# Key differences of the row maximum taken from stacked halves of k and from q over minus q, and q's row pairs added by a reduction

## The chip, the cores and the metric

The kernel runs on one core of a Trainium2 chip. The core has TensorE (PE; its weight loads are listed as PEld), VectorE (DVE), ScalarE (ACT), GpSimd (POOL), and SyncE (SP), whose queue starts nearly all DMAs here. The metric is the device time of one execution in microseconds, the median of several runs.

## The reference

```python
def _attn_ref(q, k, v):                       # (4, 8, 1152, 64) each
    q_pool = q.reshape(B, H, S // 2, 2, D).mean(axis=3)
    scores = scale * np.matmul(q_pool, k.transpose(0, 1, 3, 2))
    scores = scores - np.max(scores, axis=-1, keepdims=True)
    attn = np.exp(scores)
    attn = attn / (np.sum(attn, axis=-1, keepdims=True) + 1e-09)
    return np.matmul(attn, v)
def _moe_ref(x, w_gate, w_noise, noise, w1, w2):   # x (2304, 512), 8 experts, F = 1024
    noisy_logits = x @ w_gate + np.log1p(np.exp(x @ w_noise)) * noise
    top2 = ...                                # two experts per row, weights by softmax
    out[mask] += top2_w * (np.maximum(x[mask] @ w1[e], 0.0) @ w2[e])
```

q's rows are averaged in pairs, so 576 query rows of each of the 32 heads meet 1152 keys. The output of attention feeds a mixture of experts.

## The kernel before, in words

Two batch items of one head form a *pair*; there are 16, each with 1152 query rows (9 chunks of 128; the middle one, c = 4, holds the end of the first item and the start of the second) and 18 key chunks. A pair's rows are worked on in three *segments* of three chunks, 48 segments in all.

Values that need more than fp16 are split into a high half (`hi`, ScalarE, L293) and a low one (`lo`, VectorE, L290: scaled source minus high half). For a pair: SP loads the keys into `kr` (L267) and q into `qr` (L279 to L282). ScalarE and VectorE write high and low half of the keys side by side into `kn`, and a DMA transposes `kn` into `kt` (L296), so that partitions 0 to 63 of `kt` hold the high half and 64 to 127 the low one. `kt`'s upper rows are copied within SBUF into `kt2` (L454). For q, an add of the two rows of each pair gives `qs` (L462, on GpSimd or VectorE), ScalarE writes its high half twice side by side into `qn`, in one instruction, and this is transposed into `qt` (L296). The low half goes to `qn2`.

The row maximum, needed before exp, doesn't look at each score of its own. Each item's key chunks are taken as two blocks of ND = 4 chunks and one chunk of rest. `kd` is the difference of the two blocks in `kt` (`k_df`, L300, VectorE, two per pair). TensorE forms D = q.kd and S = q.(second block) (`max_mm`, L306); ScalarE writes relu(D) to `rd` (L314), and VectorE adds S and takes the maximum (L318), as max(a, b) = b + relu(a - b). A reduction (L336) adds the rest, and `max_fin` (L343 to L345) writes the negative maximum into two columns of `qn2`, which is transposed into `qt2`. In the order of instructions both this and the first transposition stand as `qt..<-qn..`: `qt_0` and `qt_1` are the buffers of `qt2`, `qn_0` and `qn_1` those of `qn2`.

Then come the scores (L358 with `qt` and `kt`, L359 with `qt2` and `kt2`, which subtracts the maximum too), exp on ScalarE into `pf` (L366), the low half `pl` of the probabilities (L371 on VectorE, one instruction of 128x768, or L374 on GpSimd, two of 128x384), the product with the values (`pv`, L394) and the division (L405 to L416). Routing scatters the rows to buffers of the experts (`xg`), which were filled with zeros from `zt` before (L683).

No instruction's place is written by hand. Class `Plan` (L114) is a list scheduler: each operation has an engine with a cost, a key (when it is wanted), a latency, buffers that it takes and gives back, and a flag `port`; operations with this flag on VectorE and on GpSimd are planned not to overlap. Where two engines are given (the sum of q, `pl`), the planner takes the one that ends first. A pair's operations are due some units before its first segment, a unit being a key chunk of a segment; that lead is 0, -6, -2, 4, 10 and 16 for the first six pairs and 20 from then on. For the first four pairs `qt2` is transposed by segments, later in one piece.

Of the kernel before, what the change touches and what calls it, by code (L numbers as in the profile page):

```python
# [14 lines left out]
ALU = mybir.AluOpType  # L15
AX = mybir.AxisListType
# [3 lines left out]
P = 128  # L20
# [4 lines left out]
NK = 9  # L25
D = 64
# [27 lines left out]
ND = 4  # L54
# [59 lines left out]
class Plan:  # L114
# [17 lines left out]
    def op(s, eng, cost, key, fn, deps=(), lat=None, port=False, take=(), give=(), ready=0.0, gen=None, after=None):  # L132
        o = Op(eng, cost, key, fn, lat, port, take, give)
        o.ready, o.gen = ready, gen
        s.hard += gen is None
        for tag in give:
            s.refs[tag] = s.refs.get(tag, 0) + 1
        for d in deps:
            if d.done is None:
                d.succ.append(o)  # L140
                o.wait += 1
            else:
                o.ready = max(o.ready, d.done)
        if after and after.done is None:
            after.then.append(o)
            o.wait += 1
        if not o.wait:
            s.can.append(o)
        return o
# [70 lines left out]
class Attn:  # L220
# [68 lines left out]
    def lo(s, out, src, scale, hi):  # L289
        s.nc.vector.scalar_tensor_tensor(out, src, scale, hi, op0=ALU.mult, op1=ALU.subtract)  # L290

    def hi(s, out, src, scale):
        s.nc.scalar.activation(out, src, AF.Copy, scale=scale)  # L293

# [1 line left out]
        s.nc.sync.dma_start_transpose(out=out, in_=src.rearrange("p c d -> p (c d)"))  # L296

    def k_df(s, i, h):
        kt = s.G.buf["kt", i].rearrange("p (b c) t -> p b c t", b=2)
        s.nc.vector.tensor_sub(s.G.buf["kd", i][:, h], kt[:, h, 0:ND], kt[:, h, ND:2 * ND])  # L300

# [116 lines left out]
    def pairs(s):  # L418

        G = s.G  # L420
        op = G.op
        B = s.G.buf
        scale = IN_SCALE
# [3 lines left out]
        for i in range(NPAIR):  # L427
            b = 27 * i
            x = i == 0
            ahead = (0, -6, -2, 4, 10, 16)[i] if i < 6 else 20  # L430
            hs = [slice(0, NK), slice(NK, 2 * NK)]
            k = lambda late, first: b - first if x else b - late - ahead * (late > 16)
            lq = []
# [3 lines left out]
            for h in range(2):  # L437
                lk.append(op("SP", 0.6, k(62, 99) + 2 * h, lambda i=i, h=h: s.load_k(i, h), lat=3.0,
                             take=[("kr", ("kr", i))] if h == 0 else (), after=lk[0] if h else None))
            lq.append(op("SP", 2.6, k(60, 95), lambda i=i: s.load_q(i, 1 if i == 0 else 2), lat=3.0,  # L440
                         take=() if x else [("qr", ("qr", i))], after=lq[0] if x else None))
            tr, df, kc = [], [], []
            hi = None
            for h, c in enumerate(hs):
                hi = op("ACT", 0.58, k(50, 90) + 4 * h, lambda i=i, c=c: s.hi(B["kn", i][:, c, 0:D], B["kr", i][:, c], scale),
                        deps=[lk[h]], take=[("kn", ("kn", i)), ("kt", ("kt", i))] if h == 0 else (), after=hi)
                lo = op("DVE", 0.67, k(48, 90) + 4 * h,
                        lambda i=i, c=c: s.lo(B["kn", i][:, c, D:], B["kr", i][:, c], scale, B["kn", i][:, c, 0:D]),
                        deps=[hi], port=True, give=[("kr", i)])
                tr.append(op("SP", 1.3 if x else 1.7, k(47, 90) + 4 * h, lambda i=i, c=c: s.transpose(B["kt", i][:, c], B["kn", i][:, c]),  # L450
                             deps=[lo], lat=2.1 if x else 3.2, give=[("kn", i)]))
                df.append(op("DVE", 0.33, k(38, 80) + 4 * h + 34 * h * x, lambda i=i, h=h: s.k_df(i, h),
                             deps=[tr[h]], port=True, take=[("kd", ("kd", i))] if h == 0 else (), after=df[0] if h else None))
                kc.append(op("SP", 0.6, k(20, 82) + 9 * h, lambda i=i, c=c: s.nc.sync.dma_start(B["kt2", i][0:D, c], B["kt", i][0:D, c]),  # L454
                             deps=[tr[h]], take=[("kt2", ("kt2", i))] if h == 0 else (), after=kc[0] if h else None))
            s.last = lq + tr
            qt, ql, a = [], [], None
            for p in ((0, 1) if x else (2,)):
                c = (slice(0, 3), slice(3, NCQ), slice(0, NCQ))[p]
                f = (c.stop - c.start) / NCQ  # L460
                a = op((("POOL", 0.1 + 1.45 * f), ("DVE", 0.07 + 0.74 * f)), 0, k(50, 92) + 8 * p * x,
                       lambda eng, i=i, c=c: (s.nc.vector if eng == "DVE" else s.nc.gpsimd).tensor_add(  # L462
                           B["qs", i][:, c], B["qr", i][:, c, 0], B["qr", i][:, c, 1]),
                       deps=[lq[p % 2]], port=True, take=[("qs", ("qs", i)), ("qn", ("qn", i)), ("qt", ("qt", i))] if p != 1 else (), after=a,
                       give=[("qr", i)])

                def q_hi(i=i, c=c):
                    m = c.stop - c.start
                    s.hi(B["qn", i][:, c].rearrange("p c (y d) -> p c y d", y=2),
                         B["qs", i][:, c, None, :].to_broadcast([P, m, 2, D]), 0.5 * scale)  # L470
                hi = op("ACT", 0.1 + 0.96 * f, k(44, 91) + 8 * p * x, q_hi, deps=[a])
                t = op("SP", 1.35, k(43, 91) + 8 * p * x, lambda i=i, c=c: s.transpose(B["qt", i][:, c], B["qn", i][:, c]), deps=[hi], lat=2.0 if x else 2.7,
                       give=[("qn", i)])
                qt.append(t)
                ql.append(op("DVE", 0.07 + 0.6 * f, k(40, 45) + 20 * p * x,
                             lambda i=i, c=c: s.lo(B["qn2", i][:, c, 0:D], B["qs", i][:, c], 0.5 * scale, B["qn", i][:, c, 0:D]),
                             deps=[hi], port=True, take=[("qn2", ("qn2", i))] if p != 1 else (), give=[("qs", i), ("qn", i)], after=ql[0] if ql else None))
            allred = []
            each = i < 4
            for g in range(3):  # L480
                m = 3 * i + g
# [4 lines left out]
                for ci in range(3):  # L486
                    c = 3 * g + ci
                    mm = op("PE", 0.62 if c == 4 else 0.43, k0 + 3 * ci, lambda i=i, c=c: s.max_mm(i, c),
                            deps=[df[h] for h in w] + [q],
                            take=[("bank", ("D", i, c)), ("bank", ("S", i, c))], give=[("kd", i)])  # L490
                    rl = op("ACT", 0.48, k0 + 3 * ci + 0.5, lambda i=i, c=c: s.max_relu(i, c), deps=[mm],
                            take=[("rd", ("rd", i, c))], give=[("D", i, c)])
                    red.append(op("DVE", 0.67, k0 + 3 * ci + 1, lambda i=i, c=c: s.max_red(i, c), deps=[rl],
                                  give=[("S", i, c), ("rd", i, c)]))
                soon = x and g == 0
                rest = op("PE", 0.39 if g == 1 else 0.17, k0 + 5 - 6 * soon, lambda i=i, g=g: s.max_rest(i, g),
                          deps=[q, tr[0]] if soon else red, take=[("wide" if soon else "bank", ("R", i, g))])
                red.append(op("DVE", 0.47, k0 + 7 - 8 * soon, lambda i=i, g=g: s.rest_red(i, g), deps=[rest], give=[("R", i, g)]))
                allred += red
                if each or g == 2:  # L500
                    c = slice(3 * g, 3 * g + 3) if each else slice(0, NCQ)
                    fin = op("DVE", 0.6, k0 + 9, lambda i=i, c=c, g=g: s.max_fin(i, c, g), deps=allred + [ql[min(g, len(ql) - 1)]],
                             give=[("R", i, g)])
                    t = op("SP", 1.35, k0 + 9, lambda i=i, c=c: s.transpose(B["qt2", i][:, c], B["qn2", i][:, c]), deps=[fin],
                           lat=2.1 if x else 3.0, take=[("qt2", ("qt2", i))] if g == 0 or not each else (), give=[("qn2", i)], after=ready[i, 0][0] if each and g else None)
# [6 lines left out]
            hi = None  # L512
            for h, c in enumerate(vs):
                hi = op("ACT", 0.1 + 0.96 / len(vs), b + 0 + 1 * h, lambda i=i, c=c: s.hi(B["vv", i][:, c, 0:D], B["vr", i][:, c], scale),
                        deps=[lv], take=[("vv", ("vv", i))] if h == 0 else (), after=hi)
                vdone[i].append(op("DVE", 0.08 + 1.2 / len(vs), b + 3 + 1 * h,
                                   lambda i=i, c=c: s.lo(B["vv", i][:, c, 65:129], B["vr", i][:, c], scale, B["vv", i][:, c, 0:D]),
                                   deps=[hi], port=True, give=[("vr", i)]))
# [743 lines left out]
```

## Time and profile before

| | us |
|---|---|
| median of 3 runs | 864.55 |
| lowest and highest of them | 862.39, 867.07 |
| the profiled execution, its own time | 864.92 |
| its span | 863.2 |

The clock granted to TensorE over the span is 0.979 of full speed. Rows are read thus: a group of instructions has its line, engine, operation, names, shapes (partitions x elements) and count, then busy time in us and the mean of one in ns, then the idle time of the engine just before them and what ended it. A wait is "who waited <- what ended it: us in total, times, longest". Stretches of time count from the start of the span; TensorE's clock is given in shares of full speed.

### The profile page before, as it was taken

To read this page: it belongs to the slowest core of one execution; us is meant where nothing else is said; L and a number is where in the kernel's file an instruction comes from. 1 tells how busy PE (TensorE), PEld (TensorE's weight loads), DVE (VectorE), ACT (ScalarE), POOL (GpSimd) and SP (SyncE) were. 2 spreads that over 40 slices of the span, in tenths; PEclk is the share of its full clock that TensorE was granted. 3 is DMA by queue.
4 is the path that set the end of the run, shared out by engine and by line. 5 is a ranking of instruction groups with operands and counts; after the bars stand their busy time and mean duration, and the time that the engine had idled before them with its cause. 6 is when DMAs were issued, how large, how long until landed. Compare 5 with 4: busy or idle time off the path is not lost.

```text
span 863.2 us, 21194 instructions
## 1 busy us (share of the span) xinstructions
PE 805.6 (93%) x8685; PEld 534.8 (62%) x8685; DVE 531.6 (62%) x1267; ACT 445.7 (52%) x670; POOL 397.8 (46%) x374
## 2 busy tenths in 40 slices
PE   4899989999999997898898999999999999999994
PEld 1667666777777775676766664565564755647442
DVE  6989888898999989899898231543142232422200
ACT  5778777878788876586454222333232333322310
POOL 4569875998788987387216212010202012030222
PEclk9999999999999999899899999999999999999998
DMA  8989988789896994538998842565628364290242
GB/s 213 205 231 197 216 224 175 175 200 214 189 206 177 199 209 116 147 105 250 169 241 288 233 76 30 158 168 146 148 74 222 73 181 99 93 203 13 29 57 39
DMA packets 216949, 137.80 MB, mean 160 GB/s; under 512 B 150544, under 2 KB 187920, under 8 KB 216848
## 3 DMA queue, kind: packets, MB, share of 16 engines
q1 hardware_dynamic: 208208, 116.33, 56.1%
q0 software_dynamic: 8640, 20.08, 11.4%
q8 instruction: 69, 1.13, 0.6%
q14 instruction: 32, 0.26, 0.1%
HBM read 62.14 MB, written 35.44 MB: 113 GB/s over the span
## 4 chain that ended last, share of the span: by engine, by line
PE 66%; DVE 20%; issue 4%; ACT 4%; DMA 3%; SPq 1%; POOL 1%; ACTq 0%; POOLq 0%; DVEq 0%
PE pss L1011 23%; PE psm L1028 22%; PE psm L394 7%; PE psm L306 5%; DVE pl L371 5%; PE pss L358 4%; PE pss L359 4%; DVE rd L318 4%; ACT pf L366 2%; DVE kn L290 1%; DVE vv L290 1%; ACT rd L314 1%; DMA kr<-in_k_dram 1%; DVE wl L962 1%; DVE kd L300 1%
## 5 line engine op out<-in xcount | busy, mean ns | idle before, releaser
L374 POOL TENSOR_TENSOR pl<-pf 128x384 f16<-128x384 f32 x272 | 267.8, 1015 | 73.7 <-ACT pf L366 62.9
L366 ACT ACTIVATE pf<-pss 128x768 f32<-128x768 f32 x216 | 173.8, 812 | 73.0 <-PE pss L359 48.3
L99 POOL DMA_INDIRECT out_dram<-y,mti x40 | 62.2, 1555 | 307.4 <-ACT y L1033 298.0
L394 PEld LDWEIGHTS <-pf 128*128 128x128 bf16 x2880 | 157.6, 99 | 41.3 <-issue 13.6
L394 PE MATMUL psm<-vv,pf 128*128 128x65 f16 (+1 forms) x2880 | 167.8, 195 | 4.8 <-DVE vv L290 2.5
L394 PE MATMUL psm<-vv,pl 128*128 128x65 f16 (+1 forms) x1440 | 158.8, 194 | 7.0 <-DVE pl L371 6.3
L358 PE MATMUL pss<-qt,kt 128*128 128x384 f16 (+1 forms) x576 | 152.0, 293 | 2.9 <-ACT pf L366 2.7
L359 PE MATMUL pss<-qt,kt 66*128 66x384 f16 (+1 forms) x576 | 152.4, 294 | 1.5 <-DMA qt<-qn 1.5
L1021 DVE SCALAR_TENSOR_TENSOR hl<-pss,hh 128x640 f16<-128x640 f32 (+1 forms) x64 | 46.3, 724 | 162.5 <-ACT hh L1020 162.5
L394 PEld LDWEIGHTS <-pl 128*128 128x128 f16 x1440 | 127.7, 100 | 11.1 <-DVE pl L371 7.4
L1028 PE MATMUL psm<-wh,hl 128*128 128x512 f16 x320 | 121.3, 379 | 0.0
L1028 PE MATMUL psm<-wl,hh 128*128 128x512 f16 x320 | 121.3, 379 | 0.0
L1028 PE MATMUL psm<-wh,hh 128*128 128x512 f16 x320 | 121.3, 379 | 0.0
L1028 PEld LDWEIGHTS <-hh 128*128 128x128 f16 x640 | 62.5, 98 | 73.8
L318 DVE CUSTOM_DVE_ANT_0 rd<-psm,rd 128x512 f32<-128x512 f32 x144 | 97.3, 683 | 16.3 <-ACT rd L314 15.3
L1033 ACT ACTIVATE y<-psm,mg 128x512 f32<-128x512 f32 x40 | 27.5, 687 | 143.7 <-issue 77.6
L1020 ACT ACTIVATE hh<-pss 128x640 f16<-128x640 f32 (+1 forms) x64 | 39.9, 623 | 119.2 <-PE pss L1011 119.2
L314 ACT ACTIVATE rd<-psm 128x512 f32<-128x512 f32 x144 | 85.7, 596 | 19.6 <-PE psm L306 17.4
L371 DVE TENSOR_TENSOR pl<-pf 128x768 f16<-128x768 f32 x80 | 92.2, 1169 | 0.5 <-ACT pf L366 0.4
L306 PE MATMUL psm<-kt,qt 128*128 128x128 f16 (+3 forms) x317 | 76.3, 313 | 9.3 <-DVE mx L318 4.8
L358 PEld LDWEIGHTS <-kt 128*128 128x128 f16 x576 | 57.6, 100 | 21.2 <-issue 8.7
L359 PEld LDWEIGHTS <-kt 66*128 66x128 f16 x576 | 57.6, 100 | 19.4 <-issue 6.0
(220 smaller groups left out, 1178.7 us busy)
## 6 DMA issues: line engine op xcount, KB each, us to landing
xg<-zt SPq DMA_DIRECT2D x40, 260.0 KB, 4.7
kr<-in_k_dram SPq DMA_DIRECT2D x32, 288.0 KB, 3.7
vr<-in_v_dram SPq DMA_DIRECT2D x16, 576.0 KB, 4.9
kr<-in_moe_w_dram SPq DMA_DIRECT2D x16, 512.0 KB, 4.1
qr<-in_moe_w_dram SPq DMA_DIRECT2D x16, 512.0 KB, 5.3
kn<-in_moe_w_dram SPq DMA_DIRECT2D x16, 512.0 KB, 4.7
qr<-in_q_dram SPq DMA_DIRECT2D x31, 256.0 KB, 3.4
vr<-in_moe_w_dram SPq DMA_DIRECT2D x14, 512.0 KB, 4.8
```

The lines of the kernel that those rows point to most:

```text
L99: i = nc.gpsimd.indirect_dma_start(out=out, out_offset=bass.IndirectOffsetOnAxis(ap=idx, axis=0), in_=src, in_offset=None, **kw)
L306: s.nc.tensor.matmul(ps[r, o:o + m.shape[1] * P], s.G.buf["qt", i][:, c, r], m, start=True, stop=True)
L314: s.nc.scalar.activation(s.G.buf["rd", i, c], s.G.buf["D", i, c], AF.Relu)
L318: s.nc.vector.tensor_tensor_reduce(out=rd, in0=s.G.buf["S", i, c], in1=rd, scale=1.0, scalar=-3.0e38, op0=ALU.add, op1=ALU.max, accum_out= ...
L358: mm(ps[:, a, o:o + w], kt[:, hh * NK + kc, :], qf[:, q0:q0 + w], start=True, stop=False)
L359: mm(ps[:, a, o:o + w], kt2[0:66, hh * NK + kc, :], qf2[0:66, q0:q0 + w], start=False, stop=True)
L366: s.nc.scalar.activation(s.parts(u)[0], s.G.buf["ps", u][:, :, 0:SG], AF.Exp, scale=0.125 / (IN_SCALE * IN_SCALE))
L371: s.nc.vector.tensor_sub(pl, pf, ph)
L374: s.nc.gpsimd.tensor_sub(pl[:, a], pf[:, a], ph[:, a])
L394: mm(o[:, 0:x], src[:, t % 2, ci * P:ci * P + P], vv[:, hh * NK + kc, a:a + x], start=st, stop=last and src is pl, skip_group_check=True)
L1011: nc.tensor.matmul(ps[:, i, 0:N], w[:, dc, f * P:(f + 1) * P], xT[:, 2 * dc + x, i * N:(i + 1) * N], start=(n == 0), stop=(n == 11))
L1028: s.nc.tensor.matmul(ps, h[:, f, b * P:(b + 1) * P], w[:, f, :], start=(f == 0 and k == 0), stop=(f == 7 and k == 2))
```

## The change

From the second pair on (`i >= 1`) the differences are no longer computed by VectorE. Two DMAs for each half copy the high halves of the first and the second block on top of one another into `kd`: partitions 0 to 63 hold the first block, 64 to 127 the second. q's high half stands in `qt` over its negative, so that the matmul with `kd` subtracts. The low half of the keys is negated, so that products with `kt` are what they were. In the difference the low half of the keys is then left out. The two halves of q are written by two instructions of ScalarE in place of one. From the second pair on the sum of q's row pairs is a reduction on VectorE, without the `port` flag; it was an add on either engine.

```diff
+    def minus_lo(s, out, src, scale, hi):
+        s.nc.vector.scalar_tensor_tensor(out, src, -scale, hi, op0=ALU.mult, op1=ALU.add)
...
     def k_df(s, i, h):
+        if i >= 1:
+            for y in range(2):
+                s.nc.sync.dma_start(s.G.buf["kd", i][64 * y:64 * y + 64, h],
+                                    s.G.buf["kt", i][0:D, h * NK + y * ND:h * NK + y * ND + ND])
+            return
         kt = s.G.buf["kt", i].rearrange("p (b c) t -> p b c t", b=2)
         s.nc.vector.tensor_sub(s.G.buf["kd", i][:, h], kt[:, h, 0:ND], kt[:, h, ND:2 * ND])
...
-                        lambda i=i, c=c: s.lo(B["kn", i][:, c, D:], B["kr", i][:, c], scale, B["kn", i][:, c, 0:D]),
+                        lambda i=i, c=c: s.minus_lo(B["kn", i][:, c, D:], B["kr", i][:, c], scale, B["kn", i][:, c, 0:D]),
...
-                df.append(op("DVE", 0.33, k(38, 80) + 4 * h + 34 * h * x, lambda i=i, h=h: s.k_df(i, h),
-                             deps=[tr[h]], port=True, take=[("kd", ("kd", i))] if h == 0 else (), after=df[0] if h else None))
+                df.append(op("SP" if i >= 1 else "DVE", 1.2 if i >= 1 else 0.33, (k(43, 80) if i >= 1 else k(38, 80)) + 4 * h + 34 * h * x, lambda i=i, h=h: s.k_df(i, h),
+                             deps=[tr[h]], port=i < 1, lat=3.0 if i >= 1 else None, take=[("kd", ("kd", i))] if h == 0 else (), after=df[0] if h else None))
...
+                else:
+                    a = op("DVE", 1.27, k(50, 92), lambda i=i: s.nc.vector.tensor_reduce(
+                               B["qs", i], B["qr", i].rearrange("p c r d -> p c d r"), axis=AX.X, op=ALU.add),
+                           deps=[lq[p % 2]], take=[("qs", ("qs", i)), ("qn", ("qn", i)), ("qt", ("qt", i))], give=[("qr", i)])
...
                 def q_hi(i=i, c=c):
-                    m = c.stop - c.start
-                    s.hi(B["qn", i][:, c].rearrange("p c (y d) -> p c y d", y=2),
-                         B["qs", i][:, c, None, :].to_broadcast([P, m, 2, D]), 0.5 * scale)
-                hi = op("ACT", 0.1 + 0.96 * f, k(44, 91) + 8 * p * x, q_hi, deps=[a])
+                    for y in range(2):
+                        s.hi(B["qn", i][:, c, D * y:D * y + D], B["qs", i][:, c], (0.5 - y) * scale)
+                hi = op("ACT", 0.2 + 0.96 * f, k(44, 91) + 8 * p * x, q_hi, deps=[a])
```

The first pair keeps its subtraction and its add as they were. Since costs and engines changed, the planner orders all of attention anew. Over the whole program VectorE's `pl` go from 80 to 91 and GpSimd's instructions for it from 272 to 250.

SP's queue before, around the transposition of the fifth pair's `qt2` (`qt_0_104`); `kt_95` belongs to the seventh pair:

```order
L296 DMA_TRANSPOSE kt_95<-kn 128x9x128 x2
L267 DMA kr<-in_k_dram 128x576 x2
L683 DMA xg<-zt 256x1x520 x3
L296 DMA_TRANSPOSE qt_0_104<-qn_0_125 128x9x128
L454 DMA kt_0_120<-kt_95 64x1152 x2
```

The same place after:

```order
L299 DMA_TRANSPOSE kt_95<-kn 128x9x128
L695 DMA xg<-zt 256x1x520
L267 DMA kr<-in_k_dram 128x576
L462 DMA kt_2_122<-kt_94 64x1152
L279 DMA qr<-in_q_dram 128x4x128
L280 DMA qr<-in_q_dram 64x128
L281 DMA qr<-in_q_dram 64x128
L282 DMA qr<-in_q_dram 128x4x128
L304 DMA kd_97<-kt_95 64x512 x4
L267 DMA kr<-in_k_dram 128x576
L695 DMA xg<-zt 256x1x520
L299 DMA_TRANSPOSE qt_0_104<-qn_0_125 128x9x128
```

Four copies into `kd` for the seventh pair, and loads of q and a copy into `kt2`, now stand between its key transposition and the fifth pair's `qt2`. Three fills stood there before, and two do now.

VectorE before, where the ninth pair's differences are formed, within the maxima of other chunks (an `ISA` row is L318's sum and maximum):

```order
L290 SCALAR_TENSOR_TENSOR qn_0_125<-qs_99,qn_123 128x9x64
L336 TENSOR_REDUCE mx<-psm_67 128x3
L318 ISA rd_106,mx<-psm_65,rd_106 128x512
L318 ISA mx 128x1
L371 TENSOR_TENSOR pl_111<-pf_110 128x768
L300 TENSOR_TENSOR kd_97<-kt_93 128x512
L318 ISA rd_107,mx<-psm_66,rd_107 128x512
L318 ISA mx 128x1
```

VectorE after, in the same neighbourhood:

```order
L476 TENSOR_REDUCE qs_99<-qr 128x576
L326 ISA rd_107,mx<-psm_67,rd_107 128x512
L326 ISA mx 128x1
L413 TENSOR_SCALAR r<-psm_66 128x3
L414 RECIPROCAL r<-r 128x3
L415 TENSOR_TENSOR psm_66<-psm_66,r 128x192
L344 TENSOR_REDUCE mx<-psm_65 128x3
L424 TENSOR_TENSOR xa_132<-psm_66,xa_132 128x3x64
L293 SCALAR_TENSOR_TENSOR kn<-kr,kn 128x9x64
L379 TENSOR_TENSOR pl_111<-pf_110 128x768
L379 TENSOR_TENSOR pl_113<-pf_112 128x768
```

The difference is gone from VectorE, the reduction of q stands there, and two `pl` follow one another.

## Rows read from the trace of the kernel before

**Rows 1.** The page's first line.
```profile
span 863.2 us, 21194 instructions
```

**Rows 2.** Stretches: us, PE, PEld, DVE, ACT, POOL busy, PEclk, DMA share, GB/s.
```profile
20.00:140.00 120.00, 107.83 (x1553) 77.17 (x1551) 105.20 (x255) 89.83 (x140) 83.79 (x86) 0.94 0.95 214
140.00:300.00 160.00, 156.88 (x2615) 119.95 (x2614) 148.39 (x327) 131.08 (x204) 139.00 (x136) 1.00 0.85 188
300.00:430.00 130.00, 114.83 (x1932) 89.57 (x1928) 119.48 (x292) 82.18 (x124) 82.60 (x79) 0.94 0.70 168
...
480.00:863.00 383.00, 370.38 (x2172) 212.25 (x2170) 107.65 (x189) 108.52 (x151) 62.37 (x41) 0.99 0.49 112
```

**Rows 3.** TensorE's waits, 20 to 140 us.
```profile
PE psm L306 <- DVE mx L318: 4.6, 10, 2.2
PE psm L306 <- ACT rd L314: 2.7, 4, 1.7
...
PE pss L359 <- DMA qt<-qn: 1.5, 2, 0.8
```

**Rows 4.** TensorE's waits, 300 to 430 us.
```profile
PE psm L394 <- DVE pl L371: 6.2, 6, 1.8
PE psm L306 <- DVE mx L318: 3.8, 5, 2.2
...
PE psm L394 <- POOL pl L374: 0.5, 2, 0.3
```

**Rows 5.** The chain of waits, 20 to 420 us, by line (cut by the profile).
```profile
by line: PE psm L394 14.7%; PE psm L306 10.5%; DVE pl L371 9.1%; PE pss L358 8.5%; PE pss L359 8.4%; DVE rd L318 7.9%; issue 7.9%; ACT pf L366 4.0%; DVE kn L290 2.9%; DVE vv L290 2.5%; ACT rd L314 2.3%; DVE kd L300 1.7%; DMA qt<-qn 1.7%; DV
```

**Rows 6.** Groups by line and shape, whole span.
```profile
L374 POOL TENSOR_TENSOR pl<-pf 128x384 f16<-128x384 f32 x272 | 267.8, 1015 | 73.7 <-ACT pf L366 62.9 <-PE psm L306 8.1 <-PE psm L394 1.5
...
L366 ACT ACTIVATE pf<-pss 128x768 f32<-128x768 f32 x216 | 173.8, 812 | 73.0 <-PE pss L359 48.3 <-PE psm L394 13.6 <-POOL pl L374 2.8
...
L371 DVE TENSOR_TENSOR pl<-pf 128x768 f16<-128x768 f32 x80 | 92.2, 1169 | 0.5 <-ACT pf L366 0.4
...
L290 DVE SCALAR_TENSOR_TENSOR kn<-kr,kn 128x576 f16<-128x576 f32 x32 | 32.8, 1033 | 2.1 <-ACT kn L293 2.0
...
L290 DVE SCALAR_TENSOR_TENSOR vv<-vr,vv 128x1152 f16<-128x1152 f32 x15 | 26.7, 1781 | 0.0
...
L336 DVE TENSOR_REDUCE mx<-psm 128x3 f32<-128x384 f32 x47 | 25.9, 550 | 5.4 <-PE psm L306 5.2
...
L293 ACT ACTIVATE kn<-kr 128x576 f16<-128x576 f32 x32 | 21.8, 682 | 6.4 <-DMA kr<-in_k_dram 6.3
...
L300 DVE TENSOR_TENSOR kd<-kt 128x512 f16<-128x512 f16 x32 | 20.7, 653 | 1.7 <-DMA kt<-kn 1.6
...
L293 ACT ACTIVATE qn<-qs 128x1152 f16<-128x1152 f32 x15 | 17.4, 1162 | 0.7 <-DVE qs L462 0.4 <-POOL qs L462 0.3
...
L462 POOL TENSOR_TENSOR qs<-qr 128x576 f32<-128x576 f32 x9 | 14.1, 1567 | 19.8 <-DVE mx L318 9.9 <-DVE qn L290 9.9
...
L462 DVE TENSOR_TENSOR qs<-qr 128x576 f32<-128x576 f32 x6 | 6.7, 1110 | 0.0
...
L843 DVE TENSOR_REDUCE rta<-rua 128x18 f32<-128x144 f32 x1 | 0.3, 302 | 0.0
```

**Rows 7.** `pl` by line: shortest, median and longest in ns, first and last start.
```profile
L371 DVE TENSOR_TENSOR pl<-pf x80: 941/952/2144, 24.6 to 425.3; 128x768 f16<-128x768 f32 x80
...
L374 POOL TENSOR_TENSOR pl<-pf x272: 817/826/2328, 29.9 to 421.2; 128x384 f16<-128x384 f32 x136
```

**Rows 8.** DMA issues: count, KB each, us from issue to landing.
```profile
kt<-kt SPq DMA_DIRECT2D x32, 144.0 KB, 4.5
```

**Rows 9.** Timeline around the fifth pair's `qt2`: start, us.
```profile
124.71 1.96 SPq L683 DMA_DIRECT2D xg<-zt  x3
...
126.77 2.36 SPq L296 DMA_TRANSPOSE qt<-qn  x1
...
133.62 0.32 PE L359 MATMUL pss<-qt,kt 66*128 66x384 f16 x1 [0.83 <-DMA qt<-qn]
```

More of the change, by code (lines that the diff above doesn't have):

```diff
@@ L460, in pairs @@
                 f = (c.stop - c.start) / NCQ
[L461 to L465, printed above, removed]
+                if x:
+                    a = op((("POOL", 0.1 + 1.45 * f), ("DVE", 0.07 + 0.74 * f)), 0, k(50, 92) + 8 * p * x,
+                           lambda eng, i=i, c=c: (s.nc.vector if eng == "DVE" else s.nc.gpsimd).tensor_add(
+                               B["qs", i][:, c], B["qr", i][:, c, 0], B["qr", i][:, c, 1]),
+                           deps=[lq[p % 2]], port=True, take=[("qs", ("qs", i)), ("qn", ("qn", i)), ("qt", ("qt", i))] if p != 1 else (), after=a,
+                           give=[("qr", i)])
+                else:
+                    a = op("DVE", 1.27, k(50, 92), lambda i=i: s.nc.vector.tensor_reduce(
+                               B["qs", i], B["qr", i].rearrange("p c r d -> p c d r"), axis=AX.X, op=ALU.add),
+                           deps=[lq[p % 2]], take=[("qs", ("qs", i)), ("qn", ("qn", i)), ("qt", ("qt", i))], give=[("qr", i)])
                 def q_hi(i=i, c=c):
-                    m = c.stop - c.start
-                    s.hi(B["qn", i][:, c].rearrange("p c (y d) -> p c y d", y=2),
-                         B["qs", i][:, c, None, :].to_broadcast([P, m, 2, D]), 0.5 * scale)
-                hi = op("ACT", 0.1 + 0.96 * f, k(44, 91) + 8 * p * x, q_hi, deps=[a])
+                    for y in range(2):
+                        s.hi(B["qn", i][:, c, D * y:D * y + D], B["qs", i][:, c], (0.5 - y) * scale)
+                hi = op("ACT", 0.2 + 0.96 * f, k(44, 91) + 8 * p * x, q_hi, deps=[a])
                 t = op("SP", 1.35, k(43, 91) + 8 * p * x, lambda i=i, c=c: s.transpose(B["qt", i][:, c], B["qn", i][:, c]), deps=[hi], lat=2.0 if x else 2.7,
```

## The prediction

> **What bounds the kernel now.** I read the stretches of the span first [rows 2]. Attention runs to about 430 us and has three kinds of stretch; the expert stage behind it (480 to 863 us) isn't touched, and TensorE is busy there for 370.38 of 383 us. In stretch B (140 to 300 us) TensorE is busy for 156.88 of 160 us at a granted clock of 1.00: TensorE bounds it, and no other engine can shorten it by more than 3.1 us. In A (20 to 140) TensorE idles 12.2 us and in C (300 to 430) 15.2 us, both at a mean clock of 0.94. So whatever this change brings comes out of some 27 us of idle time in A and C. TensorE does the same matmuls before and after.
>
> Then I read what TensorE waits for. In A it is the chain of the row maximum, 4.6 us for VectorE's half and 2.7 for ScalarE's, and 1.5 us for transposed q [rows 3]. In C it is VectorE: 6.2 us for the low half of the probabilities (`pl`) and 3.8 for the maximum, against 0.5 for `pl` from GpSimd [rows 4]. The chain of waits over 20 to 420 us agrees: `pl` on VectorE 9.1%, the maximum 7.9%, the split of the keys 2.9%, of the values 2.5%, the key differences 1.7% [rows 5]. These are 24.1% of 400 us, 96 us, where VectorE is busy for 105.2 + 148.4 + 119.5 = 373 us [rows 2]. About a quarter of VectorE's busy time lies on the path, then, and of the differences 6.8 of 20.7 us, a third. I take 0.3 for what a microsecond on VectorE is worth; the ends are 0.26 and 0.33.
>
> **The change part by part.** *Key differences, VectorE.* 32 subtractions become 2: 30 x 0.653 = 19.6 us off [rows 6].
>
> *q's pair sums.* 15 of them become a reduction over the pair axis, on VectorE alone. Gone are nine adds on GpSimd, 9 x 1.567 = 14.1 us, and six on VectorE, 6 x 1.110 = 6.7 us [rows 6]. No reduction of this shape ran before. Two of other sizes did: 384 elements in 550 ns, 144 in 302 ns, a slope of 1.03 ns [rows 6]; at 1152 elements that extends to 550 + 768 x 1.03 = 1.34 us. The ends are the add that it replaces, 1.110, and the widest split of 1152 elements, 1.781 [rows 6]. I take 1.34, as the reductions are the same operation: 15 x 1.34 = 20.1 us more (16.7 to 26.7).
>
> *`pl` moves.* The planner picks an engine for each `pl`. By the order of instructions GpSimd's go from 272 to 250, two to a `pl`, and VectorE's from 80 to 91. GpSimd: 22 x 1.015 = 22.3 us off; VectorE: 11 x 1.169 = 12.9 us on [rows 6]. Thus most of what the subtractions leave free is filled again.
>
> *VectorE's balance:* -19.6 - 6.7 + 20.1 + 12.9 = +6.7 us. *GpSimd's:* -14.1 - 22.3 = -36.4 us of 305 in A to C [rows 2], 12% less.
>
> *Collisions.* The same `pl` takes 0.941 us at its shortest on VectorE, 0.952 at the median and 1.169 on the mean; GpSimd's 0.817, 0.826 and 1.015 [rows 6, 7]. Few are long and the rest undisturbed: the two engines stand in each other's way at times. On VectorE that excess is 80 x 0.228 = 18.2 us for `pl` and, by the same ratio of mean to shortest, some 6 us for the split of the keys. With 12% less on GpSimd I take 24 x 0.12 = 2.9 us of it back. VectorE is then 3.8 us up, and at 0.3 the path is **1.1 us longer** (bounds: +0.0 with the reduction at 1.110, +3.1 at 1.781).
>
> *ScalarE.* 15 instructions of 1.162 us become 30 of 576 elements, which take 0.682 in the split of the keys [rows 6]: 20.5 - 17.4 = +3.0 us. ScalarE's exp and relu make up 6.3% of the chain, 25 of its 303 busy us, so **+0.2 us**.
>
> *GpSimd's waits.* TensorE waited 0.5 us for a `pl` from GpSimd in C [rows 4], and exp 2.8 us for a buffer that GpSimd held [rows 6]. With GpSimd 12% emptier I take two thirds of these 3.3 us as gone, **-2.1 us**.
>
> *The new DMAs.* Each pair from the second on copies two halves twice within SBUF, 60 copies of 64 KB on SP's queue. Nothing like a 64 KB copy into `kd` is in the trace; the nearest is the copy of `kt` into `kt2`, 144 KB, which lands 4.5 us after its issue [rows 8], against 0.653 us for the subtraction. From about the seventh pair on the planner's keys put it some 20 units ahead of its use, and that lead hides 4 us; there the copy costs nothing. The cover is gone for the first few pairs, in A, where the lead is small and the DMA engines are 0.95 busy at 214 GB/s [rows 2]. SP's issues take 1.96 / 3 = 0.65 us each where they stand in a row [rows 9]. Up to the fifth pair's second q transpose six pairs' copies stand in SP's order, 6 x 4 x 64 KB = 1.57 MB; two fills of the scatter buffer less stand ahead of it (0.53 MB): +1.0 MB, 1.0 / 0.214 = 4.9 us if the DMA engines set the pace throughout A, and 0 if the copies only fill gaps (TensorE is shown to wait for that transpose for 1.5 us of 120). I take a fifth, **+1.0 us**, with the ends 0 and +10 (second rival).
>
> **Sum:** 1.1 + 0.2 - 2.1 + 1.0 = +0.2 us. The profiled execution took 864.92 us for a span of 863.2 us [rows 1], 0.4 above the median of the runs, 864.55. With the sum on the median: **864.7 us**, no change that can be measured.
>
> **The rivals.** *(1) Faster: fewer collisions.* VectorE and GpSimd may bound A and C together. Of the work on which they are in each other's way, 19.6 + 6.7 + 36.4 go and 12.9 come, 50 us less of about 460 (`pl` 267.8 + 92.2, keys 32.8, values 26.7, differences 20.7, sums 20.8, [rows 6]), a ninth; whether the reduction takes part in it the trace of before doesn't show. TensorE's waits for VectorE, ScalarE and GpSimd that are shown in A and C are 4.6 + 2.7 + 6.2 + 3.8 + 0.5 = 17.8 us [rows 3, 4]. If half of them go, 864.9 - 8.9 = **856 us**; if nearly all, 850. For it: `pl`'s mean of 1.169 against 0.941, the longest lasting over twice the shortest [rows 7]. Against it: in C the wait is for VectorE, which gets 11 more `pl`, some of them there, and the medians lie at the shortest times. The Trainium skill's page "SBUF — State Buffer", section "Who interferes with whom", states the rule behind this rival: a VectorE instruction with two inputs from SBUF and a GpSimd one that reads SBUF exclude each other for the whole instruction, and a reduction never takes part. Single `pl` stretched to 2144 ns agree with it, medians at the shortest time don't ask for it; by the rule alone the time would be this rival's, without it the sum's.
>
> *(2) Slower: SP's queue in A.* Ahead of the fifth pair's second q transpose four new copies of a later pair now stand, which wait for that pair's key transpose, and the transpose queues behind them. Before, it was already late: issued at 126.77 us behind three fills, and TensorE started the score that needed it at 133.62 with a wait of 0.83 [rows 9]. If each of the second to fifth pairs pays four issues, 4 x 4 x 0.65 = 10.4 us, less two fills that went behind, 1.3: 864.7 + 9.1 = **874 us**; with two of them, 869. It decides from the point at which a transposed q or a `kd` copy lands after the matmul could have begun; TensorE's waits for DMAs in A, 1.5 us before, would then be near 10. Against it: the planner reserves 1.2 us of SP and 3.0 us to land for each pair of copies, and other waits of TensorE in A run at the same time.
>
> *(3) It doesn't do what it says.* VectorE isn't relieved, since the reduction and eleven `pl` take the room. My own sum says that already; with a reduction of 2.2 us, twice an add, VectorE is 13 us further up, at 0.3 3.9 us: 868.6. It leaves the forecast as it is.
>
> **How the numbers follow.** A measurement of this kernel can tell about 0.5%, 4.3 us, from no change. The forecast, 864.7 with a range of its own of 860.3 to 869 (third rival in it): 0.37. Port relief, 850 to 860.2: 0.34. SP's queue, 869 to 876: 0.29. The range reaches to 853 and 873, so that about one in ten is left out at either end.
>
> **What would show it.** The mean of the reduction near 1.34 us (1.11 to 1.78). VectorE busy in 20 to 430 us at 373 + 4, GpSimd at 305 - 36. Mean `pl` on VectorE below 1.169: if it falls under 1.08 and TensorE's 17.8 us of waits halve, the collisions were worth more than my 2.9 us. TensorE's waits for DMAs in A: at 1 to 3 us the new copies are hidden; near 10 the second rival holds. B stays at 3 us of idle time. The expert stage has to be as long as before; if it isn't, what I took for untouched was touched, and the forecast is wrong for a reason that isn't here. I am wrong above all if a copy into `kd` is late for many pairs and not the first alone, since each costs TensorE the difference between 4.5 us and 0.65.

## The result, and the profile after

The changed kernel takes **870.07 us** (median of 8 runs, 867.4 to 872.2) against 864.39 us for the kernel before on the same chip: a ratio of **1.007, with a 95% interval of 1.0051 to 1.009**. On another chip, which was slower for both, the ratio was 1.003 (1.0004 to 1.0056). The profiled execution has a span of 869.6 us, 6.4 us more than before [rows 1].

The stretches of the changed kernel, with the columns of [rows 2]:

```profile
20.00:140.00 120.00, 101.97 (x1510) 72.32 (x1508) 100.70 (x240) 84.59 (x137) 70.03 (x76) 0.93 0.90 200
140.00:300.00 160.00, 157.66 (x2543) 118.53 (x2542) 148.01 (x330) 131.79 (x213) 105.69 (x116) 0.99 0.98 211
300.00:430.00 130.00, 116.11 (x1956) 89.62 (x1955) 119.99 (x290) 85.52 (x129) 77.08 (x76) 0.96 0.74 180
```

The loss is in A (20 to 140 us): TensorE idles 18.0 us there, before 12.2. In B (140 to 300) and C (300 to 430) its idle time falls, from 3.1 to 2.3 and from 15.2 to 13.9. GpSimd has lost a sixth of its work, and VectorE isn't busier than before.

How far the work has come at a given time tells where a loss arises. Each of the 48 segments ends with one reciprocal of its division (L406 before, L414 after), so its start in the timeline is a milestone:

| reciprocal of the | before | after | difference |
|---|---|---|---|
| 10th segment | 116.88 | 119.29 | +2.4 |
| 12th | 132.12 | 132.04 | -0.1 |
| 13th | 147.31 | 158.34 | +11.0 |
| 30th | 279.00 | 285.89 | +6.9 |
| 48th | 427.17 | 433.22 | +6.1 |

So the milestone slips by 11 us between the 12th and 13th segments, where the fifth pair begins, and 5 come back up to the last. From there to the end of the span both take 436 us (863.2 - 427.2 and 869.6 - 433.2): the expert stage is as long as it was.

A milestone is not yet a loss, since the planner may let TensorE do other work first. TensorE's idle time up to it is the surer measure. Up to the 13th segment, before and after (columns of [rows 2]):

```profile
0.00:147.31 147.31, 123.18 (x1696) 86.05 (x1697) 123.24 (x301) 107.91 (x166) 97.99 (x107) 0.95 0.91 208
```
```profile
0.00:158.34 158.34, 127.58 (x1735) 86.15 (x1736) 127.81 (x303) 109.64 (x178) 86.17 (x100) 0.94 0.91 207
```

TensorE has idled 24.1 us before and 30.8 after, 6.6 more. In the other 4.4 of the 11 us it was busy, partly with matmuls that the kernel before does later, partly at a lower clock: in the changed kernel it is busy for 4.0 of the 8 us from 126 to 134, and from 134 to 144 its granted clock is 0.50, the lower of its two levels (1.2 GHz); before, the mean clock from 134 to 144 is 0.83. At the 30th and the 48th segment the difference in idle time is 5.3 us. So of the 5 us that come back 1.3 are idle time, and the rest is in busy time: work done ahead, and the clock.

What is late there? Rows from the timelines of SP, ScalarE, VectorE and TensorE of the changed kernel (start, us, and in brackets the idle time before):

```profile
120.97 1.42 DVE L293 SCALAR_TENSOR_TENSOR kn<-kr,kn 128x576 f16<-128x576 f32 x2
```
```profile
132.87 0.60 SPq L267 DMA_DIRECT2D kr<-in_k_dram  x1
...
136.75 2.42 SPq L304 DMA_DIRECT2D kd<-kt  x4
...
140.52 2.17 SPq L299 DMA_TRANSPOSE qt<-qn  x1
```
```profile
136.92 0.68 ACT L296 ACTIVATE kn<-kr 128x576 f16<-128x576 f32 x1 [3.94 <-DMA kr<-in_k_dram]
137.51 1.06 ACT L322 ACTIVATE rd<-psm 128x512 f32<-128x512 f32 x2
```
```profile
138.14 0.97 PE L314 MATMUL psm<-kt,qt 128*128 128x512 f16 x4 [3.13 <-ACT rd L322]
```
```profile
134.17 0.20 DVE L353 SCALAR_TENSOR_TENSOR qn<-psm,qn 128x9 f16<-128x9 f32 x1
```

Read from the top. The split of keys that frees `kr` ends at 122.4 us; SP issues the next load of `kr` at 132.87, 10.5 us later, since its entries follow one another without a gap until then. What stands there are two fills, three loads for the routing and three transpositions (7.2 us of the 10.5), and no copy into `kd`; the last four copies before it were issued from 113.8 to 116.3. ScalarE reaches the split of that load at 133, waits 3.94 us for it, and the relu behind it can't pass. TensorE's next maximum waits 3.13 us for that relu. The second thing that is late is the fifth pair's `qt2`: its input is ready at 134.4, and it is issued at 140.52, 6.2 us later, behind the load, a copy into `kt2`, four loads of q, four new copies (2.42 us) and two more. Before, it was issued 2.5 us after its input, which was ready at 124.3 us (the issue is in [rows 9]):

```profile
124.09 0.20 DVE L345 SCALAR_TENSOR_TENSOR qn<-psm,qn 128x9 f16<-128x9 f32 x1
```

ScalarE's waits for DMAs, 20 to 350 us, before and after (in total, times, longest):

```profile
ACT kn L293 <- DMA kr<-in_k_dram: 4.4, 4, 1.9
```
```profile
ACT kn L296 <- DMA kr<-in_k_dram: 11.6, 11, 3.9
ACT vv L296 <- DMA vr<-in_v_dram: 8.5, 5, 3.9
```

These waits go from 4.4 to 20.1 us. TensorE's own waits for DMAs in A hardly move: 1.5 before, 1.7 after (1.5 of these at a matmul of `kd` and `qt`, with a load named that it doesn't read). SP's entries in the timeline, whose joined rows (x2, x3) hold short gaps too, fill 54.5 and 48.8 of 60 us before (20 to 80, 80 to 140) and 56.7 and 57.2 after; from 140 to 220 it is 53.9 and then 71.9 of 80. SP's queue is all but full from 20 us on. The Trainium skill's page "Perfetto Trace Analysis", section "What 'DMA-bound' means", lists this as a limit of its own, beside the DMA engines: the issuing engine's track solid with issues. The trace agrees, with 57.2 of 60 us.

The groups that answer to [rows 6]:

```profile
L382 POOL TENSOR_TENSOR pl<-pf 128x384 f16<-128x384 f32 x250 | 230.7, 952 | 154.9 <-ACT pf L374 133.0 <-PE psm L314 14.7 <-PE psm L402 3.4
...
L379 DVE TENSOR_TENSOR pl<-pf 128x768 f16<-128x768 f32 x91 | 100.2, 1118 | 3.3 <-ACT pf L374 3.0
...
L293 DVE SCALAR_TENSOR_TENSOR kn<-kr,kn 128x576 f16<-128x576 f32 x32 | 29.5, 928 | 1.4 <-ACT kn L296 1.3
...
L290 DVE SCALAR_TENSOR_TENSOR vv<-vr,vv 128x1152 f16<-128x1152 f32 x15 | 21.8, 1451 | 0.0
L476 DVE TENSOR_REDUCE qs<-qr 128x576 f32<-128x1152 f32 x15 | 20.6, 1374 | 0.6 <-DMA qr<-in_q_dram 0.6
```

The copies themselves land soon, 2.8 us after the issue at the median, and issue like any other DMA; the row gives SP's issue time (shortest, median, longest in ns):

```profile
L304 SPq DMA_DIRECT2D kd<-kt x60: 461/594/2109, 28.1 to 364.5; - x60
```

### The profile page after: what moved, and what is told of

It is laid out like the page before. It is cut to its first block, busy times and chain, and to the rows that moved or that the text cites. A ratio compares the mean times of both kernels' runs of the same rounds, so it can differ in the third digit from the quotient of the medians.

```text
span 869.6 us, 21254 instructions
## 1 busy us (share of the span) xinstructions
PE 806.5 (93%) x8685; PEld 532.0 (61%) x8685; DVE 530.1 (61%) x1257; ACT 446.0 (51%) x687; POOL 345.4 (40%) x343
## 3 DMA queue, kind: packets, MB, share of 16 engines
q1 hardware_dynamic: 213008, 120.27, 58.3%
## 5 line engine op out<-in xcount | busy, mean ns | idle before, releaser
L382 POOL TENSOR_TENSOR pl<-pf 128x384 f16<-128x384 f32 x250 | 230.7, 952 | 154.9 <-ACT pf L374 133.0
L402 PEld LDWEIGHTS <-pf 128*128 128x128 bf16 x2880 | 156.0, 98 | 42.8 <-issue 14.5
L379 DVE TENSOR_TENSOR pl<-pf 128x768 f16<-128x768 f32 x91 | 100.2, 1118 | 3.3 <-ACT pf L374 3.0
L314 PE MATMUL psm<-kt,qt 128*128 128x128 f16 (+3 forms) x317 | 78.2, 322 | 12.0 <-DVE mx L326 5.8
```

What stands on the lines that cost most here:

```text
L314: s.nc.tensor.matmul(ps[r, o:o + m.shape[1] * P], s.G.buf["qt", i][:, c, r], m, start=True, stop=True)
L379: s.nc.vector.tensor_sub(pl, pf, ph)
L382: s.nc.gpsimd.tensor_sub(pl[:, a], pf[:, a], ph[:, a])
L402: mm(o[:, 0:x], src[:, t % 2, ci * P:ci * P + P], vv[:, hh * NK + kc, a:a + x], start=st, stop=last and src is pl, skip_group_check=True)
```

## The experiments

The theory that the runs were to test: the 60 copies cost by their issues on SP's full queue, which makes the loads behind them late, and ScalarE, which works in order, hands the delay on to TensorE. The rivals: the sum of q, now on VectorE alone; the copies' landing or bytes; and the new order that the planner makes of any change. The runs were made in four groups, each on one chip; the kernel before took 864.4, 876.7, 877.8 and 864.8 us there (the last section tells where that comes from). A ratio alone can therefore mislead between groups, and the milestones stand beside it, with TensorE's idle time up to the 13th segment (the milestone less TensorE's busy time until then). The first group is the comparison of before and after; the second holds the next four kernels of the table, the third those named so, the copies by ScalarE and the cost of 1.45, the fourth the last four.

| kernel | us | ratio to before (95%) | 13th | idle to 13th | 30th | 48th | ScalarE's waits for DMAs, 20:350 |
|---|---|---|---|---|---|---|---|
| before, first group | 864.4 |  | 147.3 | 24.1 | 279.0 | 427.2 | 4.4 |
| before, third group | 876.2 |  | 145.5 | 23.5 | 277.2 | 438.5 | 6.7 |
| after, first group | 870.1 | 1.007 (1.0051 to 1.009) | 158.3 | 30.8 | 285.9 | 433.2 | 20.1 |
| after, third group | 879.9 | 1.003 (1.0004 to 1.0056) | 157.5 | 29.4 | 284.5 | 441.8 | 19.2 |
| subtractions again | 864.2 | 0.986 (0.9844 to 0.9872) | 149.5 | 25.9 | 279.8 | 427.2 | 6.0 |
| add again | 873.0 | 0.997 (0.9954 to 0.998) | 157.0 | 30.3 | 285.2 | 435.2 | 21.3 |
| copies from pair 7 on | 870.4 | 0.993 (0.9898 to 0.9965) | 150.8 | 25.5 | 280.8 | 432.9 | 12.3 |
| two copies for a pair | 887.3 | 1.014 (1.010 to 1.0176) | 162.5 | 31.7 | 291.0 | 447.7 | 13.0 |
| copies by ScalarE | 887.5 | 1.010 (1.0066 to 1.0136) | 158.8 | 31.8 | 290.6 | 445.3 | 17.5 |
| before, cost 1.45 | 873.4 | 0.994 (0.9917 to 0.9969) | 144.5 | 24.6 | 288.6 | 433.6 | 3.5 |
| after, fills late | 878.9 | 1.016 (1.0131 to 1.0185) | 155.0 | 28.2 | 285.3 | 443.6 | 20.8 |
| subtractions, fills late | 870.8 | 1.006 (1.0032 to 1.0078) | 148.0 | 26.1 | 280.9 | 432.3 | 5.8 |
| before, fills late | 869.1 | 1.005 (1.003 to 1.0064) | 150.0 | 24.7 | 282.4 | 432.8 | 9.3 |
| before, 60 small DMAs | 883.4 | 1.020 (1.0164 to 1.0233) | 155.1 | 25.9 | 294.2 | 445.9 | 11.5 |

The idle time parts the kernels cleanly. With copies for the early pairs it is 28.2 to 31.8 us in six traces; without them it is 23.5 to 26.1 in eight, whatever the planner's order. So the early loss goes with the copies, or with the places that the planner gives them, and not with the reduction or with a new order as such. By which way they cost is the harder question, and the runs below answer it in part only.

**One part undone at a time.** The subtractions put back:

```diff
-        if i >= 1:
+        if i >= 99:
             for y in range(2):
                 s.nc.sync.dma_start(s.G.buf["kd", i][64 * y:64 * y + 64, h],
```

> The changed kernel with the key differences of all pairs by VectorE's subtraction again; the reduction for q's sum, the two instructions of ScalarE and the negated low half stay. Queue theory (the copies fill SP's queue between 20 and 140 us, and the fifth pair's second q transpose is issued 6 us after its input is ready): SP has 60 issues less, the late issue is gone, 862 to 866 us. Reduction theory (q's sum, now on VectorE alone, is what costs): stays at 868 to 872.

Measured: 864.21 us; the fifth pair's second transposition is issued 2.6 us after its input, and ScalarE's waits are back at 6.0 us. The add put back:

```diff
-                if x:
+                if True:
                     a = op((("POOL", 0.1 + 1.45 * f), ("DVE", 0.07 + 0.74 * f)), 0, k(50, 92) + 8 * p * x,
```

> The changed kernel with q's sum as an add on GpSimd or VectorE again, as the planner chooses; the copies stay. Queue theory: SP's queue is as full as in the changed kernel, 868 to 873 us. Reduction theory: back at 862 to 866.

Measured: 872.95 us, and the issue 8.8 us after its input. At the 30th segment the four combinations are 279.0 (neither part), 279.8 (reduction alone), 285.2 (copies alone) and 285.9 (both): the reduction costs 0.8 us there, the copies 6.2, together 6.9. In idle time up to the 13th they are 24.1, 25.9, 30.3 and 30.8. The ratios of these two can't be taken at their word, because in their group the kernel before was 12 us slower than in the first, for a reason of its own; the ranges in microseconds, too, were set for the first chip. The parts' order, copies dear and reduction cheap, rests on the idle time and on the two times, 864.2 and 873.0, taken on one chip.

**Copies for late pairs alone.**

```diff
-        if i >= 1:
+        if i >= 6:
             for y in range(2):
                 s.nc.sync.dma_start(s.G.buf["kd", i][64 * y:64 * y + 64, h],
```

> The changed kernel with copies from the seventh pair on only; the first six subtract. Queue theory, with the loss in the early stretch alone: the 20 copies of pairs two to six are gone from the stretch up to 140 us (four of the seventh pair's stay), 862 to 866 us, and the fifth pair's second q transpose is issued within 3 us of its input. If the copies cost all along (each late by its landing), most of the loss stays: 867 to 870. Reduction theory: 868 to 872.

The early loss is gone: the 13th segment comes at 150.8 us. The transposition is still issued 4.4 us after its input, not under 3 as expected. The gain doesn't last to the end. In the last part of attention TensorE has one wait of 4.9 us for the end of a division (L424), and the single runs spread from 863.85 to 876.72. So the early stretch is where the copies of the early pairs cost, but the total didn't follow: 870.4 us lies in the range that was given for the reduction.

**Half of the issues, the same bytes.** One copy for both halves of the keys, two for a pair:

```diff
-                s.nc.sync.dma_start(s.G.buf["kd", i][64 * y:64 * y + 64, h],
-                                    s.G.buf["kt", i][0:D, h * NK + y * ND:h * NK + y * ND + ND])
+                s.nc.sync.dma_start(kd[64 * y:64 * y + 64], kt[0:D, :, y * ND:y * ND + ND])   # both h
```

> The changed kernel with two copies for a pair, each for both halves (128 KB), in place of four of 64 KB: the same bytes, 30 issues less; a pair's first copies wait for its second key transpose. Queue theory: half of the loss comes back, 865 to 868 us. If bytes or the wait for a landing cost and not the issues: 869 to 873.

Slower than either answer: 887.3 us. ScalarE waits less (13.0), but now TensorE waits for the copies themselves (20 to 350 us):

```profile
PE psm L314 <- DMA kd<-kt: 6.2, 3, 2.6
```

A joined copy can't start before the second key transposition, and these 6.2 us are what that lateness shows. Between the 30th and the 42nd segment the kernel takes 123.0 us, the changed one 110.6; why is open. The run doesn't separate issues from bytes as it was meant to.

**The copies on ScalarE's queue.**

```diff
-                s.nc.sync.dma_start(s.G.buf["kd", i][64 * y:64 * y + 64, h],
+                s.nc.scalar.dma_start(s.G.buf["kd", i][64 * y:64 * y + 64, h],
```

> The changed kernel with the 60 copies issued by ScalarE's queue, the plan knowing it. Queue theory: SP has its 60 issues less, the fifth pair's second q transpose is issued within 3 us of its input, and the time is that of the first experiment (subtractions, reduction kept), 862 to 866 us. If the copies' bytes or their landing are what costs: 868 to 872. If an issue on ScalarE takes as long as on SP (0.6 us), ScalarE is 36 us busier, and exp is late: 866 to 872 with waits for exp in place of waits behind SP's queue.

887.52 us; SP is relieved (the transposition waits 0.9 us, and ScalarE's waits for loads of k and v are 4.0 us), and ScalarE pays. Its timeline around 134 us:

```profile
134.54 4.29 ACTq L304 DMA_DIRECT2D kd<-kt  x2
138.88 0.60 ACT L322 ACTIVATE rd<-psm 128x512 f32<-128x512 f32 x1 [4.66 <-DMA xg<-zt]
```

TensorE's next matmul of the maximum waits 3.36 us for that relu.

The two copies take 0.47 and 0.48 us; in the 3.3 us between them the second waits, and relu and exp behind it. What it waits for is named in the relu's row: a zero fill (`xg`), which SP issued at 132.27 us. The copy uses the same semaphore as that fill (a counter that tells of a DMA's landing). In every trace eight such semaphores go round among the DMAs of SP and ScalarE, so a DMA can be held until one some eight issues ahead has landed. In all, ScalarE's relu waits 13.5 us behind copies, of which 4.9 end with a transposition of keys. The third expectation had the right engine, but not the reason: an issue there takes 0.48 us at the median, and the waits before the issues cost more.

**The order alone.** The kernel before with one cost of the planner changed; one `pl` goes to GpSimd by it, and nothing else is computed otherwise:

```diff
-            pls[u] = op((("POOL", 1.43), ("DVE", 0.87)), 0, 2 * u + 2, lambda eng, u=u: s.p_lo(u, eng), deps=[ex[u]], port=True)
+            pls[u] = op((("POOL", 1.45), ("DVE", 0.87)), 0, 2 * u + 2, lambda eng, u=u: s.p_lo(u, eng), deps=[ex[u]], port=True)
```

> The kernel before with one number of the plan moved: the cost that the planner reckons for a low half of the probabilities on GpSimd, 1.43 to 1.45. Nothing that is computed changes, the order does in many places. It shows how far the order alone moves the time. Queue theory: SP's issues are as many, so within 0.3% of the kernel before. If the order is what decides: differences of the size of the change, 6 us either way.

Its 30th segment comes at 288.6 us, 11.4 later than in the kernel before on the same chip, and its total (outside the 0.3% that the queue theory gave) is 0.6% below that kernel's: the 42nd segment is still 4.1 us later, and the gain comes behind it, where the kernel before loses on that chip (last section). So the order moves the time by as much as the change does, and a loss of 6 us alone proves no cause. What tells the copies' loss from this one is its place and its waits: this kernel's 13th segment is early (144.5), with 24.6 us of idle time, ScalarE's waits for DMAs are 3.5 us, and it loses in B by waits for the maximum (5.6 us, before 1.8). All six traces of kernels with copies on SP (the changed one twice, the add again, the late pairs, two for a pair, the late fills) have 12.3 to 21.3 us of these waits; without copies and without added issues they are 3.5 to 9.3.

**Issues without bytes.** The kernel before with 60 DMAs of 8 bytes where the changed kernel has its copies; nobody waits for them:

```diff
+    def dummy(s, i, h):
+        for y in range(2):
+            x = 4 * i + 2 * h + y
+            s.nc.sync.dma_start(s.dum[0:1, 4 * x:4 * x + 4], s.G.buf["kt", i][0:1, h * NK + y * ND, 0:4])
...
+                if i >= 1:
+                    op("SP", 1.2, k(43, 80) + 4 * h, lambda i=i, h=h: s.dummy(i, h), deps=[tr[h]], lat=3.0, give=[("kt", i)])
```

> The kernel before with 60 more DMAs on SP's queue that carry 8 bytes each, put where the changed kernel has its copies, with the copies' cost in the plan and nobody waiting for them; the subtractions stay. Queue theory: the issues alone cost, the 13th segment comes at 153 to 160 us, and the time is 1.004 to 1.012 of the kernel before. If the bytes, or TensorE's wait for a copy's landing, are what costs: the 13th segment at 147 to 150 and 0.998 to 1.003.

The 13th segment comes at 155.1, within the 153 to 160 expected, and the total is 1.020, more than was expected. SP's entries fill 57.1 of 60 us between 80 and 140. But the place is another. TensorE's busy time up to the 13th segment:

```profile
0.00:155.11 155.11, 129.25 (x1786) 90.59 (x1787) 124.19 (x302) 108.34 (x167) 96.42 (x110) 0.93 0.87 198
```

It has idled 25.9 us by then, 1.7 more than before and not 6.6. The 12th segment, at 144.2 us, is already 12.1 us late, which in the changed kernel it isn't. TensorE idles in B, for 10.4 us (3.1 before), 6.5 of them in waits for the maximum, as with the order alone. ScalarE's waits for DMAs rise to 11.5 us, so with the issues loads do come late; that this makes TensorE idle as in the changed kernel the run doesn't show. That the milestone met the theory's range is luck: it got there by another way. The issues cost as much time on SP as the copies' own:

```profile
L306 SPq DMA_DIRECT2D dum<-kt x60: 567/616/1226, 25.7 to 370.4; - x60
```

A DMA of 8 bytes holds SP's queue for 616 ns, one of 64 KB for 594: an issue's time doesn't grow with the bytes. For such a limit the same section of the Trainium skill's "Perfetto Trace Analysis" names large descriptors as what matters; in these two rows the DMA's size made no difference to the issue.

**Room made on SP.** The fills of the scatter buffers, 40 issues, released from 150 us on, in three kernels:

```diff
-            op("SP", 0.6, 20 + 4.7 * x, lambda x=x: R.zero(s.zt, *divmod(x, NB)), deps=[s.set], ready=30.0 + 4.2 * x)
+            op("SP", 0.6, 20 + 4.7 * x, lambda x=x: R.zero(s.zt, *divmod(x, NB)), deps=[s.set], ready=150.0 + 2.8 * x)
```

In the changed kernel:

> The changed kernel with the zero fills of the scatter buffers, 40 issues of SP, released to the plan from 150 us on and not from 30 us on. Queue theory: SP has some 20 issues of 0.65 us less in the early stretch, the fifth pair's second q transpose waits less than 3 us in the queue, and the reciprocal of the 13th segment, at 147 us in the kernel before and at 158 in the changed one, comes at 145 to 150; the time is 5 to 10 us below the changed kernel's. If the copies cost by their landing, or the planner's order does: the 13th segment stays at 155 or later.

With the subtractions:

> The kernel of the first experiment (subtractions by VectorE, q's sum by the reduction) with the fills from 150 us on as well. Queue theory: the early stretch has the least on SP's queue of all kernels, the 13th segment at 140 to 147 us, and the time is 0.98 to 0.985 of the kernel before. If SP's queue isn't the limit there: 0.986 as in the first experiment.

In the kernel before:

> The kernel before with the fills from 150 us on. Queue theory: SP was already 0.9 busy in its early stretch, so it gains a little too, 0.99 to 0.998 of the kernel before, with the 13th segment at 142 to 147 us; less than the changed kernel gains. If the fills are harmless: 1.00.

All three were slower than expected. The changed kernel's transposition waits 2.7 us in place of 6.2, and its 13th segment comes 3.4 us sooner, not 8 to 13: at 154.97 us it lies at the rivals' 155, and the idle time up to it falls from 30.8 to 28.2, by less than half of the excess. The 24th comes 5.6 us sooner (236.66 to 242.27), but the 48th 10.3 us later. SP's entries now fill 76.8 of 80 us between 220 and 300 (67.7 without the move), and 76.1 in the kernel before (58.3): the moved fills make SP as full there as it was early. In the kernel before, SP's entries between 80 and 140 fall from 48.8 to 36.6 us, and TensorE's idle time up to the 13th segment stays (24.1 and 24.7). Without the copies SP's queue isn't the limit there. Where the fifth pair's remaining lateness comes from (its maximum is ready at 135.2 us, before 124.3) these runs don't settle: the planner's order differs there as well.

## Why the prediction was right, and where it failed

The time lay in the range, and on the side that the second rival had with 0.29; the forecast of no measurable change, at 0.37, missed by 5.4 us and just beyond its own range. The sum had +0.2 us where the kernel lost 5.7, so the hit is owed to the width of the range.

- **The reduction:** 1.34 us by the slope of two other reductions; measured 1.374 (the row of L476 above). The subtractions left VectorE as reckoned, 20.7 to 0.8 us.
- **Collisions** were the term on VectorE that was too small. I took back 2.9 us. Work that stayed the same got shorter by 12.8: 91 `pl` by 0.051 us each (4.6), the values' split from 1.781 to 1.451 us each (4.9), the keys' from 32.8 to 29.5 in all (3.3); only q's got longer, from 14.5 to 15.4. VectorE in 20 to 430 us went from 373.1 to 368.7, down 4.4, not up 3.8. GpSimd fell by 52.6 us, not 36.4, since its `pl` fell to 952 ns as well. The first rival's mechanism is there, then, if less surely than the sum says: in the kernels that compute as before and differ in order, fills or small DMAs the means move too (`pl` on VectorE 1138 to 1240 ns, the values 1561 to 1781, the keys 864 to 1033); only GpSimd's `pl` (1004 to 1034) stay clear of the 952. Its own sign, a mean `pl` below 1.08 us, didn't come (1.118). What it was worth to TensorE is seen at most in the 1.3 us of idle time that come back after the 13th segment; that link wasn't tested by itself.
- **GpSimd's waits:** exp's wait for it went from 2.8 to 2.5 us, and TensorE's in C rose from 0.5 to 1.9. The -2.1 us (two thirds of 3.3 are 2.2) didn't come.
- **The new DMAs** are the term that was mis-sized: +1.0 us was taken, and TensorE idles 6.6 us more up to the 13th segment and 5.3 up to the 30th. The place was named rightly, the queue's way at the fifth pair's `qt2` too (four copies at 0.65 us; measured 2.42 for the four, 6.2 in all). Wrong was to cost only what lands late for TensorE and to leave out the loads of other pairs behind a queue with entries in 54.5 of 60 us already before. In the timeline a late load holds ScalarE for 3.94 us and TensorE for 3.13. How much of the 6.6 us goes this way isn't shown: 60 small DMAs made loads late and TensorE hardly idler there (25.9 us), and with SP relieved of the fills the changed kernel kept 28.2.
- **The sign to look for** misled, and the second rival's range was met without it: TensorE's waits for DMAs in A stayed at 1.7 us, which I had written down as "hidden". The waits stand one engine further up, on ScalarE, 20.1 us (20 to 350), and TensorE's row names ScalarE's relu.
- **B and the expert stage** behaved as said: 2.3 us of idle time, and 436 us from the last segment on.

What is shown is that with copies for the early pairs TensorE has idled 28.2 to 31.8 us up to the 13th segment, and 23.5 to 26.1 without them. What stays open is by which way they cost (SP's issues, the wait for a landing, or where the planner puts them), and how much of the total's 6 us they are, since one cost of 1.45 moves the milestones as far.

## What to carry to other kernels

Before work is moved from a busy engine to DMAs, add up the issuing queue's own timeline: an issue holds it for about 0.6 us here, with 8 bytes as with 64 KB, and a queue at 0.9 delays what stands behind. A late load shows where it is first used in order, here on ScalarE, so look at the waits for DMAs of every engine and not of TensorE alone. Measure a loss by TensorE's idle time and not by a milestone alone, which a new order shifts too: 60 small DMAs met the expected milestone and lost elsewhere. With a planner in between, run a control that changes the order and nothing else before a difference of under 1% is put down to a cause.

## What the runs showed of the hardware

The kernel before and the changed one were run once more on one chip:

> The kernel before, unchanged, to have its trace from the same chip as the runs beside it. On the first chip it took 864.4 us, on the chip of the first four experiments 876.7. If its time follows the chip, the trace should show one place where a DMA lands later and TensorE waits longer; if nothing differs, it will be 862 to 867 us again.

> The changed kernel, unchanged, a second time. If the change costs whatever the chip, the ratio to the kernel before is 1.005 to 1.009 again. If the kernel before is the one that depends on the chip and the changed one doesn't (870 us), the ratio is below 1 where the kernel before is at 876, and 1.007 where it is at 864.

The kernel before took 876.2 us there, and 864.4 in the first group, although its work was equally far up to the 42nd segment (390.71 and 391.47 us). The changed kernel took 879.9; neither of its expectations held quite, as both kernels depend on the chip. The difference arises while GpSimd sends out the scatters of the first half. The stretch from 395 to 400 us, in that run and in the first (columns of [rows 2]):

```profile
395.00:400.00 5.00, 2.53 (x20) 1.52 (x18) 0.00 (x0) 0.81 (x1) 3.78 (x5) 0.50 0.82 318
```
```profile
395.00:400.00 5.00, 5.00 (x97) 3.92 (x94) 4.93 (x9) 4.47 (x7) 4.08 (x4) 1.00 0.94 355
```

On the slower chip VectorE does nothing in these 5 us, TensorE is half idle at a granted clock of 0.50, the lower of its two levels (1.2 GHz), and of its waits from 380 to 440 us 4.1 us have no releaser in the profile ("issue"), where the first chip's trace has none of this kind.

The changed kernel shows such waits there too (5.2 us; 13th segment 157.5, 48th 441.8 against 433.2). The kernel with the subtractions put back ran at 864.2 us on a chip on which the kernel before took 876.7; that it misses such a stall by its timing is a guess. Its cause wasn't tried, and whether that kernel is better than the one before on every chip is open.
